# A fused attention, GLU and MLP kernel on one core: the second block's split moved ahead of the last half product, a third staging tile, other places for token sums and weight work

## The chip, the cores and the metric

One NeuronCore of one Trainium2 chip runs the whole program. The metric is the device time of one execution in microseconds, as the median of the runs; lower is better. The names of the engines are those of the profile: PE (TensorE), DVE (VectorE), ACT (ScalarE), POOL (GpSimd), SP (SyncE, here a queue for DMAs).

## What is computed

```python
phi = lambda x: exp(h - max(h)) / sqrt(128)        # h = x @ omega.T - |x|^2 / 2
x  = attention(phi(q), phi(k), v)                  # (4, 8, 576, 64) -> 2304 tokens x 512
xn = x / sqrt(mean(x * x) + 1e-6) * rms_g
x  = (silu(xn @ w_gate) * (xn @ w_val)) @ w_out    # 512 -> 1536 -> 512, the GLU
out = silu(x @ w2_in) @ w2_out                     # 512 -> 2048 -> 512, the MLP
```

All data are float32. A product of two float32 matrices is made of three passes of a rounded type (high times high, high times low, low times high), so every operand is split once into a high part (an ACT copy that rounds) and a low part (a DVE subtraction).

## The kernel before

The 2304 tokens are five blocks: 0 to 3 of 512 tokens and block 4 of 256. Behind the attention, `stream()` (L748) writes out the order of the GLU's and MLP's work as a generator; each `yield` ends a piece of PE work of a known length, and the weight queue `wq` uses these lengths to place its own jobs (decoding a weight tile on DVE, L146 to L157, adding its two halves on POOL, L160, scaling it on ACT, L168, splitting it on ACT L457 and DVE L461, adding weight tiles on POOL, L357). A call of `wq.tick()` issues one job. All engines take their instructions in the order in which they are issued.

The GLU's hidden width is cut in twelve tiles `f`. The first three are done block by block ("the third f", in the order 1, 0, 2, 3, 4); the other nine, u = 0 to 8, go by `quad()` (L593), which makes gate and value of two blocks at once, for blocks 0 and 1 (p = 0) and then for blocks 2 and 3 (p = 1), with seven half products (L595, six matmuls of 128x512 each) in place of eight; for this it needs sums of the tokens' halves (`token_sums`, L365: L382 the low parts, L379 the high ones, L387 and L390 the sums) and of the weights. In a quad the two blocks' results are `t11` and `t12`; L627 adds, L622 is the silu, L685 is `t12 * t22` of the second block where p = 1, L693 the same product where p = 0, L690 is `t11 * pb` of the first block, and L198 (ACT) and L199 (DVE) are the split of the result in `hs`. L607 copies a partial sum of one PSUM tile into the next, which the following half product continues. Block 4 has its own `glu_block` (L205 matmuls, L719 silu, L716 product, and the split is put off in a list `wait` until the next quad's first half product).

A result tile `hs` then goes through the output weights: `g2_glu` (L247, matmuls L264), four pieces of 12 or 6 matmuls for each block; other work is woven between the pieces (`more()`, `pend`). Blocks 3 and 4 are added up in SBUF (L284, DVE). Blocks 0, 1 and 2 have no room there: a piece is copied from PSUM to a staging tile (L275 on ACT, L277 on DVE, two pieces in one tile) and a POOL DMA adds it to a copy in DRAM (`kept`, L278). There are two staging tiles, used in turn, so a copy waits until the DMA that read its tile two earlier is done. Behind the last GLU group the copies come back to SBUF as the MLP's input; L254 splits them. The MLP's first group, "std", is done block by block.

Of the kernel before, what the change touches and what calls it, by code (L numbers as in the profile page):

```python
# [20 lines left out]
def kernel(  # L21
# [84 lines left out]
    f = 0  # L106
# [140 lines left out]
    def g2_glu(fs, j, hs, first, last):  # L247
        wq.need(*[(1, "o", f) for f in fs])
        staged = j < NE and not last
# [9 lines left out]
        for d in range(KC):  # L259
# [12 lines left out]
            if staged:  # L272
                if d % 2 == 0:
                    o = stage()
                    nc.scalar.activation(out=o[:, 0, :], in_=ps, func=AF.Copy)  # L275
                else:
                    nc.vector.tensor_copy(out=o[:, 1, :], in_=ps)  # L277
                    nc.gpsimd.dma_start(  # L278
                        out=kept(j, d // 2), in_=o.rearrange("p t d -> p (t d)"), accum_op=ALU.add
                    )  # L280
            elif first:
                nc.scalar.activation(out=y[:, d, :], in_=ps, func=AF.Copy)
            else:
                nc.vector.tensor_tensor(out=y[:, d, :], in0=ps, in1=y[:, d, :], op=ALU.add)  # L284
            if last:
# [78 lines left out]
    def token_sums(p, temp, end, eng=nc.vector):  # L364
# [3 lines left out]
        def tok_high(n, x):  # L368
            if n == 1:
                tok[p, n] = [xs[2 * p + 1][:, a, :KH, :] for a in range(2)]  # L370
            elif p:
                v = big.tile([P, KC * TB * P], F32R, tag=f"ya{n - 2}", name=f"ya{n - 2}")
# [40 lines left out]
    class WeightQueue:  # L413
# [28 lines left out]
        def plan(self, u):  # L442
# [82 lines left out]
            elif std <= u < std + NSTD:  # L525
# [8 lines left out]
                    (0, lambda: dec(bs[1], 1), lambda: load(u + 1, 1, 1)),  # L534
                    (1, lambda: hi(a0)),
                    (0, lambda: lo(a0)),
                    (0, lambda: dec(bs[0], 0), lambda: load(u + 1, 0, 0)),
# [63 lines left out]
    def quad(u, ys, hs, p=0, skip=0, done=True):  # L601
# [41 lines left out]
        while wait:  # L643
            wait.pop(0)()
# [25 lines left out]
        if kind == 2:  # L670
            silu(t22, t22)
            hs[j1][fs[1]] = split_h(t22, j1)
        yield from more(gap)
# [5 lines left out]
        silu(t12, t12)  # L679
        if kind == 2:  # L680
            hs[j1][fs[0]] = split_h(t12, j1)
        wq.tick()
        yield from more(gap)
        if kind == 1 and p:
            nc.vector.tensor_tensor(out=t12, in0=t12, in1=t22, op=ALU.mult)  # L685
            hs[j1][fs[0]] = split_h(t12, j1)
        yield step
        product(w2, KH, summed(p, 4), pb, False)
        if kind == 1:
            nc.vector.tensor_tensor(out=t11, in0=t11, in1=pb, op=ALU.mult)  # L690
            hs[j0][fs[0]] = split_h(t11, j0)
            if not p:
                nc.vector.tensor_tensor(out=t12, in0=t12, in1=t22, op=ALU.mult)  # L693
            yield from ys
            if not p:
                hs[j1][fs[0]] = split_h(t12, j1)
# [4 lines left out]
        wq.tick()  # L701
# [43 lines left out]

    def chain_of(*its):
# [3 lines left out]
    def stream():  # L750
        f0, (f2,) = sweeps[0][1], sweeps[1][1]
        for j in range(NE):
            for n in range(2):
                nc.sync.dma_start(out=kept(j, n), in_=ya[j][:, 1024 * n:1024 * (n + 1)])
        pend = ()
        order = [(3, f0), (4, f0), (1, [f2]), (0, [f2]), (2, [f2]), (3, [f2]), (4, [f2])]
# [20 lines left out]
        for n, (j, fs) in enumerate(order):  # L777
            hs, mine = {}, n == len(order) - 1
            for f in fs:
                yield from g1_glu(f, j, hs, () if mine else pend)  # L780
                pend = pend if mine else ()
            if n == 2:
                sums.extend(later)
                wq.free += [(0, k) for k in range(6)]
                wq.slot(("t", 1))
                stages[:] = [wq.slot(("y", k), F32) for k in range(2)]
                wq.held["t", 0] = 1, 1
                now, later = sums23()
                sums.extend(now[:9])
            out = g2_glu(fs, j, hs, j >= NE and fs is f0, False)  # L790
            pend = chain_of(pend, out) if mine else out
        sums.extend(now[9:] + later)
        wq.free.append((1, 0))
        for u, (kind, fs) in enumerate(groups):
# [6 lines left out]
            if std <= u < std + NSTD:  # L801
# [40 lines left out]
                continue  # L842
            yield from quad(u, iter(pend), hs, int(done), done=False)
# [4 lines left out]
            if kind == 1:  # L848
                out_of = lambda j: g2_glu(fs, j, hs[j], False, done)
                if done:  # L850
                    wq.release(("y", 0), ("y", 1))
                    for j in (2, 0, 1):
# [834 lines left out]
```

## Time and profile before

| | |
|---|---|
| median of 3 runs | 992.53 us (993.13, 989.47, 992.53) |
| the profiled execution | 991.23 us, of which its span 989.5 us |
| PE busy | 942.9 us, 95% |
| DVE, ACT, POOL busy | 711.3, 527.9, 470.6 us |
| mean granted TensorE clock | 0.985 |

The page's rows give for each engine its busy time, and for each wait the engine and line that ended it. A timeline row gives the start, the length, the engine, the line, output and inputs, the count, and in brackets the idle time in front of it with what ended it. PEclk is the granted TensorE clock as a share of full speed, 2.4 GHz; at 0.50 it is 1.2 GHz.

### The profile page before, as it was taken

The page shows a single profiled execution, that of the slowest core. Times are in us where ns is not written, and L with a number is a line of the kernel's source. Part 1 is how long each engine was busy: PE and PEld are TensorE (multiplying, and loading weights), DVE is VectorE, ACT ScalarE, POOL GpSimd, SP SyncE. Part 2 cuts the span into 40 slices and gives each one's busy share as a digit, 9 for nine tenths or more (in the row PEclk, how much of TensorE's full clock was granted, in tenths as well). Part 3 has the DMA queues.
Part 4 walks back from the last instruction along what each step waited for, and adds up shares of the span by engine and source line. Part 5 has one row for each costly group of instructions (what it writes and reads, how often), then busy time and mean ns, then how long its engine had stood idle before and what let it go on. Part 6 is the DMA issues. An engine that isn't in the chain of part 4 may idle for free.

```text
span 989.5 us, 17410 instructions
## 1 busy us (share of the span) xinstructions
PE 942.9 (95%) x6480; PEld 778.8 (79%) x6480; DVE 711.3 (72%) x1329; ACT 527.9 (53%) x1151; POOL 470.6 (48%) x495
## 2 busy tenths in 40 slices
PE   8999999999789999999999979999999999999998
PEld 6888878887577777777777757888888888888886
DVE  6998999658666876776776687989666666575633
ACT  6999786544344444354454435565645454545442
POOL 8887744335334344344344332636445454454411
PEclk9999999998899999999999989999999999999999
DMA  7654445137038367367467561355777786878777
GB/s 193 162 145 130 133 129 166 46 83 151 22 68 183 81 121 172 80 127 167 89 128 158 107 203 43 107 174 103 160 135 158 122 170 125 170 134 170 112 150 163
DMA packets 98789, 129.66 MB, mean 131 GB/s; under 512 B 29456, under 2 KB 75792, under 8 KB 98704
## 3 DMA queue, kind: packets, MB, share of 16 engines
q0 software_dynamic: 17280, 59.78, 34.6%
q1 hardware_dynamic: 81152, 68.70, 24.1%
q8 instruction: 51, 0.84, 0.4%
q14 instruction: 34, 0.28, 0.1%
q10 hardware_dynamic: 272, 0.07, 0.0%
HBM read 54.59 MB, written 69.21 MB: 125 GB/s over the span
## 4 chain that ended last, share of the span: by engine, by line
PE 74%; DVE 11%; ACT 5%; issue 4%; DMA 4%; POOL 1%; SPq 1%; DVEq 0%; POOLq 0%; ACTq 0%
PE g L595 23%; PE y L314 20%; PE y L264 8%; PE g L205 6%; PE y L205 3%; PE b L1155 3%; DMA out_dram<-w 3%; PE b L205 2%; ACT h L198 2%; PE b L1555 2%; PE b L1339 2%; PE kv L1235 1%; DVE w L461 1%; DVE h L199 1%; PE b L1128 1%
## 5 line engine op out<-in xcount | busy, mean ns | idle before, releaser
L160 POOL TENSOR_TENSOR m<-m,raw 128x512 int32<-128x512 int32 x136 | 198.2, 1458 | 232.7 <-DVE m L157 141.1
L314 PE MATMUL y<-w,h 128*128 128x512 f32 (+1 forms) x870 | 212.1, 388 | 0.2 <-ACT h L198 0.2
L595 PE MATMUL g<-xs,w 128*128 128x512 f32 x720 | 186.3, 396 | 7.4 <-DVE xs L382 6.2
L314 PEld LDWEIGHTS y<-w,h 128*128 128x128 f32 x870 | 161.9, 188 | 34.3 <-ACT h L198 0.7
L264 PE MATMUL y<-h,w 128*128 128x512 f32 (+1 forms) x648 | 158.9, 377 | 12.3 <-DVE h L199 4.0
L199 DVE TENSOR_TENSOR h<-s,h 128x512 fp32r<-128x512 f32 (+1 forms) x134 | 107.9, 815 | 83.8 <-ACT h L198 83.1
L595 PEld LDWEIGHTS g<-xs,w 128*128 128x128 f32 x720 | 136.3, 191 | 36.7 <-DVE xs L382 6.5
L264 PEld LDWEIGHTS y<-h,w 128*128 128x128 f32 x648 | 115.0, 192 | 44.0 <-DVE h L199 7.0
L198 ACT ACTIVATE h<-s 128x512 fp32r<-128x512 f32 (+1 forms) x134 | 77.8, 585 | 81.4 <-DVE s L690 32.5
L339 POOL DMA_DIRECT2D out_dram<-ya x64 | 58.9, 981 | 118.0 <-DVE ya L333 49.3
L205 PE MATMUL g<-xs,w 128*128 128x512 f32 x336 | 82.3, 396 | 4.1 <-ACT w L457 4.1
L461 DVE TENSOR_TENSOR w<-m,w 128x512 fp32r<-128x512 f32 x74 | 71.3, 964 | 19.3 <-ACT w L457 19.3
L331 ACT ACTIVATE ya<-y 128x512 f32<-128x512 f32 x82 | 48.2, 594 | 69.3 <-PE y L314 62.1
L278 POOL DMA_DIRECT2D out_dram<-w x54 | 48.6, 900 | 68.4 <-ACT w L275 25.9
L1204 ACT ACTIVATE e<-b,nb 128x128 f32<-128x128 f32 x272 | 75.8, 422 | 7.6 <-issue 4.2
L595 PE MATMUL g<-ya,w 128*128 128x512 f32 x270 | 69.8, 394 | 9.4 <-ACT g L607 9.4
L333 DVE COPY ya<-y 128x512 f32<-128x512 f32 x52 | 35.8, 688 | 58.7 <-PE y L314 58.7
L205 PEld LDWEIGHTS g<-xs,w 128*128 128x128 f32 x336 | 63.9, 192 | 17.7 <-ACT w L457 4.3
L595 PE MATMUL g<-w,w 128*128 128x512 f32 x270 | 70.2, 396 | 4.6 <-ACT g L607 4.6
L607 ACT ACTIVATE g<-g 128x512 f32<-128x512 f32 x60 | 34.9, 582 | 70.2 <-PE g L595 69.6
L622 ACT ACTIVATE s<-s 128x512 f32<-128x512 f32 x42 | 26.6, 632 | 83.8 <-DVE s L627 83.8
L595 PEld LDWEIGHTS g<-ya,w 128*128 128x128 f32 x270 | 50.5, 189 | 22.6 <-ACT g L607 12.3
(137 smaller groups left out, 1570.3 us busy)
## 6 DMA issues: line engine op xcount, KB each, us to landing
out_dram<-w POOLq DMA_DIRECT2D x56, 512.0 KB, 6.8
out_dram<-ya POOLq DMA_DIRECT2D x52, 512.0 KB, 6.8
raw<-in_moe_w_out_dram SPq DMA_DIRECT2D x28, 512.0 KB, 4.3
raw<-in_moe_w_in_dram SPq DMA_DIRECT2D x16, 512.0 KB, 4.3
out_dram<-ya SPq DMA_DIRECT2D x14, 512.0 KB, 4.9
raw<-in_moe_w_gate_dram SPq DMA_DIRECT2D x12, 512.0 KB, 4.2
raw<-in_moe_w_val_dram SPq DMA_DIRECT2D x12, 512.0 KB, 4.2
qT<-e SPq DMA_DIRECT2D x72, 64.0 KB, 2.4
```

Of the source, the lines that this page charges most:

```text
L160: tt(out=mi, in0=mi, in1=(low if step == 5 else high).bitcast(I32), op=ALU.add)
L198: nc.scalar.activation(out=ht[:, 0, :], in_=s, func=AF.Copy)
L199: nc.vector.tensor_tensor(out=ht[:, 1, :], in0=s, in1=ht[:, 0, :].bitcast(F32), op=ALU.subtract)
L205: nc.tensor.matmul(out=ps, lhsT=w[:, a, cc * P:(cc + 1) * P], rhs=xs[j][:, c, cc, :], start=(n == 0), stop=(n == 3 * KC - 1),)
L264: nc.tensor.matmul(out=ps, lhsT=wt[1, "o", f][:, a, d * P:(d + 1) * P], rhs=hs[f][:, c, :], start=(n == 0), stop=(n == nn - 1),)
L278: nc.gpsimd.dma_start(out=kept(j, d // 2), in_=o.rearrange("p t d -> p (t d)"), accum_op=ALU.add)
L314: nc.tensor.matmul(out=ps, lhsT=hs[f][:, a, t * P:(t + 1) * P], rhs=wt[2, "p", f][:, c, d0:d1], start=(n == 0), stop=(n == nn - 1),)
L331: nc.scalar.activation(out=o[:, t % 2, :], in_=ps, func=AF.Copy)
L339: nc.gpsimd.dma_start(out=rows, in_=o[p0:p1], accum_op=ALU.add)
L461: eng.tensor_tensor(out=v[:, 1, :], in0=x, in1=v[:, 0, :].bitcast(F32), op=ALU.subtract)
L595: nc.tensor.matmul(out=ps, lhsT=w[:, a, (c0 + c) * P:(c0 + c + 1) * P], rhs=x(b, c), start=(start and n == 0), stop=(n == 3 * KH - 1), ski ...
L1204: nc.scalar.activation(out=st.e[r][:, :, h, :] if blocks4 else st.e[r][:, h, :], in_=src.rearrange("p (a f) -> p a f", a=4) if blocks4 els ...
```

## The change

1. The third f's output of block 1 is added in SBUF (four L284) as block 3's is, and stored by two plain POOL DMAs; only blocks 0 and 2 are stored at the start of `stream()`, and block 1's two staged accumulations at that place are gone.
2. The sums of tokens of blocks 2 and 3 are issued one block sooner (at `n == 1`), into tiles that are free there, with other tags; those of blocks 0 and 1 that are left stand in front of them, and `wq.rest` is 1.3 and then 2.1.
3. In `quad`, `t12 * t22` and the split of the second block stand right behind the sixth half product for both p. Before, for p = 0, the product stood behind the seventh half product and the first block's split, and the split behind the output pieces. The weight job that stood behind the sixth half product stands behind the fifth, and that at the quad's end is issued in fewer cases.
4. There are three staging tiles from u = 1 on instead of two. Block 4's split stands behind block 1's output pieces, and the pieces of a group come in the order 1, 2, 4 instead of 1, 4, 2; in the last GLU group the order of blocks is 2, 1, 0, 4 instead of 2, 0, 1, 4.
5. In std the decode of a second output weight tile stands one split later.

Where the lines moved: L595, L607, L622, L627, L690 and L693, L457, L461, L379, L382, L387, L390 of before are L599, L611, L626, L631, L693 and L685, L460, L464, L382, L385, L390, L393 of the changed kernel. PE has the same instructions.

DVE, where the third f of block 1 is put out and that of block 0 computed (`ya_96`: block 1's output in SBUF; `w_1` and `w_2`: staging tiles; `ya_97`: token sums; L228 and L199: block 0's product and its low part, for which PE waits). Before:

```order
L277 COPY w_1_3947<-y 128x512
L382 TENSOR_TENSOR xs_91<-raw_3715,xs_91 128x1024
L146 TENSOR_SCALAR m_3979<-raw_3911 128x512
L149 TENSOR_SCALAR raw_3911<-raw_3911 128x512
L152 TENSOR_SCALAR m_3979<-m_3979 128x512
L154 TENSOR_SCALAR raw_3911<-raw_3911 128x512
L157 TENSOR_SCALAR m_3979<-m_3979 128x512
L277 COPY w_2_3948<-y 128x512
L387 TENSOR_TENSOR ya_97<-xs_93 128x1024
L228 TENSOR_TENSOR s<-s,g 128x512
L199 TENSOR_TENSOR h<-s,h 128x512
```

DVE at the same place in the changed kernel (`w_1` is a sum of tokens here):

```order
L284 TENSOR_TENSOR ya_96<-y,ya_96 128x512
L385 TENSOR_TENSOR xs_91<-raw_3713,xs_91 128x1024
L146 TENSOR_SCALAR m_3977<-raw_3903 128x512
L149 TENSOR_SCALAR raw_3903<-raw_3903 128x512
L152 TENSOR_SCALAR m_3977<-m_3977 128x512
L154 TENSOR_SCALAR raw_3903<-raw_3903 128x512
L157 TENSOR_SCALAR m_3977<-m_3977 128x512
L284 TENSOR_TENSOR ya_96<-y,ya_96 128x512 x3
L393 TENSOR_TENSOR ya_97<-ya_97 128x1024
L393 TENSOR_TENSOR ya_97<-ya_97,w_1_3922 128x1024
L228 TENSOR_TENSOR s<-s,g 128x512
L199 TENSOR_TENSOR h<-s,h 128x512
```

Two staging copies are four additions now, and two sums of 128x1024 stand in front of block 0's product in place of one.

DVE in one period of the nine GLU groups (u = 4), first quad, from the second of the two additions (L627) on; `raw` and `m` are a weight tile before and after its decode. Before:

```order
L627 TENSOR_TENSOR s<-g,e 128x512
L461 TENSOR_TENSOR w_3_5561<-m_5479,w_3_5561 128x512
L146 TENSOR_SCALAR m_5601<-raw_5283 128x512
L149 TENSOR_SCALAR raw_5283<-raw_5283 128x512
L152 TENSOR_SCALAR m_5601<-m_5601 128x512
L154 TENSOR_SCALAR raw_5283<-raw_5283 128x512
L157 TENSOR_SCALAR m_5601<-m_5601 128x512
L277 COPY w_1_3947<-y 128x512
L690 TENSOR_TENSOR s<-s,g 128x512
L199 TENSOR_TENSOR h<-s,h 128x512
L693 TENSOR_TENSOR s<-s 128x512
L277 COPY w_2_3948<-y 128x512
```

DVE in the changed kernel, from behind the first of the two additions (L631) on; `ya_3690` is block 4's output:

```order
L464 TENSOR_TENSOR w_5_5558<-m_5479,w_5_5558 128x512
L146 TENSOR_SCALAR m_5583<-raw_5265 128x512
L149 TENSOR_SCALAR raw_5265<-raw_5265 128x512
L152 TENSOR_SCALAR m_5583<-m_5583 128x512
L154 TENSOR_SCALAR raw_5265<-raw_5265 128x512
L157 TENSOR_SCALAR m_5583<-m_5583 128x512
L277 COPY w_0_4520<-y 128x512
L631 TENSOR_TENSOR s<-g,e 128x512
L685 TENSOR_TENSOR s<-s 128x512
L199 TENSOR_TENSOR h<-s,h 128x512
L284 TENSOR_TENSOR ya_3690<-y,ya_3690 128x256 x2
L693 TENSOR_TENSOR s<-s,g 128x512
```

The decode (L146 to L157) and its split, which stood behind both additions, stand in front of the second, and the second block's product and low part (L685, L199) are in front of the first block's (L693, L199) and no longer behind.

ACT in the same period, second quad, from two staging copies (L275) to block 4's silu (L719). Before:

```order
L275 ACTIVATE w_1_3947<-y 128x512
L275 ACTIVATE w_2_3948<-y 128x512
L622 ACTIVATE s<-s 128x512
L168 ACTIVATE m_5647<-m_5647,g_sb 128x128 x4
L457 ACTIVATE w_1_5741<-m_5647 128x512
L198 ACTIVATE h<-s 128x512 x2
L719 ACTIVATE s<-y 128x256
```

ACT at the same place in the changed kernel (L626 is the second silu):

```order
L275 ACTIVATE w_2_3951<-y 128x512
L168 ACTIVATE m_5647<-m_5647,g_sb 128x128 x4
L460 ACTIVATE w_0_5721<-m_5647 128x512
L275 ACTIVATE w_3_3952<-y 128x512
L626 ACTIVATE s<-s 128x512
L198 ACTIVATE h<-s 128x512 x2
L719 ACTIVATE s<-y 128x256
```

The scaling of a weight tile (L168 four times) and its high part (L460), which stood between the second silu and the two L198, stand in front of that silu.

The core of the diff:

```diff
     def g2_glu(fs, j, hs, first, last, keep=None):
-        staged = j < NE and not last
+        staged = j < NE and not last and keep is None
...
+            if keep and d % 2:
+                keep(j, d // 2)
...
     def tok_high(n, x):
             elif p:
-                v = big.tile([P, KC * TB * P], F32R, tag=f"ya{n - 2}", name=f"ya{n - 2}")
+                tag = f"ya{(1, 0, 2)[n - 2]}"
+                v = big.tile([P, KC * TB * P], F32R, tag=tag, name=tag)
...
     def quad(u, ys, hs, p=0, skip=0, done=True):
         product(w1, 0, half(0, 0), pa, True)
         copy(pb, pa)
-        while wait:
-            wait.pop(0)()
...
         product(s34, 0, summed(p, 3), pb, False)
         t22 = plus(pb)
         if kind == 2:
             silu(t22, t22)
             hs[j1][fs[1]] = split_h(t22, j1)
+        else:
+            wq.tick()
         yield from more(gap)
         yield step
         product(s34, KH, half(1, KH), pc, False)
...
         t12 = plus(pc)
         silu(t12, t12)
+        if kind == 1:
+            nc.vector.tensor_tensor(out=t12, in0=t12, in1=t22, op=ALU.mult)
+        hs[j1][fs[0]] = split_h(t12, j1)
         if kind == 2:
-            hs[j1][fs[0]] = split_h(t12, j1)
-        wq.tick()
+            wq.tick()
         yield from more(gap)
-        if kind == 1 and p:
-            nc.vector.tensor_tensor(out=t12, in0=t12, in1=t22, op=ALU.mult)
-            hs[j1][fs[0]] = split_h(t12, j1)
         yield step
         product(w2, KH, summed(p, 4), pb, False)
         if kind == 1:
             nc.vector.tensor_tensor(out=t11, in0=t11, in1=pb, op=ALU.mult)
             hs[j0][fs[0]] = split_h(t11, j0)
-            if not p:
-                nc.vector.tensor_tensor(out=t12, in0=t12, in1=t22, op=ALU.mult)
             yield from ys
-            if not p:
-                hs[j1][fs[0]] = split_h(t12, j1)
...
-        wq.tick()
+        if kind == 2 or not done:
+            wq.tick()
...
     def stream():
-        for j in range(NE):
+        for j in (0, 2):
...
+        wq.rest = 1.3
...
-            wq.rest = T_PACE if wq.hold else S_REST
+            wq.rest = 2.1
...
+            if n == 1:
+                wq.free += [(0, k) for k in range(4)]
+                for k in range(2):
+                    wq.slot(("t", k), F32)
+                now, later23 = sums23()
+                sums.extend(now)
             if n == 2:
-                sums.extend(later)
+                sums[:0] = later
...
-                sums.extend(now[:9])
+            if n == 5:
+                sums.extend(later23)
...
+            if u == 1:
+                stages.insert(0, wq.slot(("y", 2), F32))
...
                 yield from glu_block(fs[0], 4, hs[4], iter(()), {"g": 0, "v": 0})
+                wq.tick()
                 if done:
-                    pend = chain_of(*map(out_of, (2, 0, 1, 4)))
+                    pend = chain_of(*map(out_of, (2, 1, 0, 4)))
                 else:
                     yield from out_of(3)
-                    pend = chain_of(*map(out_of, (2, 1, 4) if u + 2 == std else (1, 4, 2)))
+                    pend = chain_of(out_of(1), flush(), out_of(2), out_of(4))
```

## Rows read from the trace of the kernel before

**Rows 1.** The page's busy times: engine, us, share of the span, instructions.

```profile
PE 942.9 (95%) x6480; PEld 778.8 (79%) x6480; DVE 711.3 (72%) x1329; ACT 527.9 (53%) x1151; POOL 470.6 (48%) x495
```

**Rows 2.** Waits of PE: what it waited for, us in total, times, longest.

```profile
PE g L595 <- ACT g L607: 14.0, 8, 4.6
PE g L595 <- DVE xs L382: 6.2, 1, 6.2
```

**Rows 3.** Timeline of PE, third f and first quads, rows with idle time in front.

```profile
219.04 0.50 PE L264 MATMUL y<-h,w 128*128 128x512 f32 x1 [0.53 <-ACT h L198]
...
229.75 0.50 PE L264 MATMUL y<-h,w 128*128 128x512 f32 x1 [1.75 <-ACT h L198]
...
230.87 3.35 PE L264 MATMUL y<-h,w 128*128 128x512 f32 x7 [0.62 <-DVE h L199]
...
264.88 2.50 PE L595 MATMUL g<-xs,w 128*128 128x512 f32 x5 [6.15 <-DVE xs L382]
...
283.33 2.06 PE L264 MATMUL y<-h,w 128*128 128x512 f32 x6 [1.93 <-ACT s L719]
```

**Rows 4.** Windows: stretch, length, busy time of each engine, then the granted clock.

```profile
230.90:237.00 6.10, 6.10 (x14) 4.76 (x15) 4.31 (x6) 2.44 (x4) 3.08 (x3) 0.50 0.93 154
...
261.50:267.10 5.60, 2.22 (x5) 1.83 (x6) 5.01 (x12) 0.00 (x0) 3.27 (x1) 0.50 0.00 0
...
284.60:288.10 3.50, 3.50 (x10) 2.77 (x9) 1.99 (x4) 0.11 (x1) 0.00 (x0) 0.54 0.00 0
...
300.00:570.00 270.00, 253.77 (x1202) 206.27 (x1201) 189.37 (x340) 121.70 (x248) 115.32 (x114) 1.00 0.61 127
574.90:581.90 7.00, 5.96 (x14) 4.70 (x15) 4.75 (x9) 3.05 (x6) 2.59 (x2) 0.51 0.18 71
```

**Rows 5.** Timeline of DVE, third f: the sum ahead of block 0's product, and that product.

```profile
215.78 1.95 DVE L387 TENSOR_TENSOR ya<-xs 128x1024 f32<-128x1024 f32 x1
217.65 0.68 DVE L228 TENSOR_TENSOR s<-s,g 128x512 f32<-128x512 f32 x1
```

**Rows 6.** Timeline of ACT, third f: the staging copy ahead of block 2's split.

```profile
226.61 0.60 ACT L275 ACTIVATE w<-y 128x512 f32<-128x512 f32 x1 [3.60 <-DMA out_dram<-w]
```

**Rows 7.** Timeline of PE in one period, from the second quad on.

```profile
421.67 1.67 PE L595 MATMUL g<-ya,w 128*128 128x512 f32 x6 [1.34 <-ACT g L607]
...
431.36 2.99 PE L205 MATMUL y<-xs,w 128*128 128x256 f32 x24
434.19 0.39 PE L264 MATMUL y<-h,w 128*128 128x512 f32 x1
...
438.74 1.54 PE L595 MATMUL g<-xs,w 128*128 128x512 f32 x6
```

**Rows 8.** Timeline of DVE in the same period, first quad's end.

```profile
413.57 0.69 DVE L627 TENSOR_TENSOR s<-g,e 128x512 f32<-128x512 f32 x1 [0.75 <-PE g L595]
...
418.43 1.43 DVE L199 TENSOR_TENSOR h<-s,h 128x512 fp32r<-128x512 f32 x1 [0.70 <-ACT h L198]
419.79 0.68 DVE L693 TENSOR_TENSOR s<-s 128x512 f32<-128x512 f32 x1
```

**Rows 9.** Timeline of POOL: the decode's pair of additions beside that L199.

```profile
416.63 2.69 POOL L160 TENSOR_TENSOR m<-m,raw 128x512 int32<-128x512 int32 x2 [6.52 <-DVE m L157]
```

**Rows 10.** Timeline of ACT in the same period: the scaling ahead of the two L198.

```profile
431.46 1.27 ACT L168 ACTIVATE m<-m,g_sb 128x128 f32<-128x128 f32 x4
432.76 0.63 ACT L457 ACTIVATE w<-m 128x512 fp32r<-128x512 f32 x1
```

**Rows 11.** Timeline of PE at the end of the GLU: its two longest waits there.

```profile
575.95 2.50 PE L595 MATMUL g<-w,w 128*128 128x512 f32 x5 [4.60 <-ACT g L607]
...
595.44 2.06 PE L205 MATMUL g<-xs,w 128*128 128x512 f32 x4 [4.08 <-ACT w L457]
```

**Rows 12.** Timeline of ACT ahead of those two: a staging copy, and the first block's split.

```profile
566.95 0.60 ACT L275 ACTIVATE w<-y 128x512 f32<-128x512 f32 x1 [1.87 <-DMA out_dram<-w]
...
594.24 0.63 ACT L198 ACTIVATE h<-s 128x512 fp32r<-128x512 f32 x1 [2.44 <-DVE s L693]
```

More of the change, by code (lines that the diff above doesn't have):

```diff
@@ L245, in kept, with g2_glu @@
         return out[r0:r0 + 2 * P, :].rearrange("(p r) d -> p (r d)", r=2)
-    def g2_glu(fs, j, hs, first, last):
+    def g2_glu(fs, j, hs, first, last, keep=None):
         wq.need(*[(1, "o", f) for f in fs])
-        staged = j < NE and not last
+        staged = j < NE and not last and keep is None
         y = ya[j].rearrange("p (c t) -> p c t", c=KC)
@@ L533, in plan @@
                     (0, lambda: lo(a1)),
-                    (0, lambda: dec(bs[1], 1), lambda: load(u + 1, 1, 1)),
+                    *[(0, lambda: dec(bs[1], 1), lambda: load(u + 1, 1, 1))] * (u > std),
                     (1, lambda: hi(a0)),
                     (0, lambda: lo(a0)),
+                    *[(0, lambda: dec(bs[1], 1), lambda: load(u + 1, 1, 1))] * (u == std),
                     (0, lambda: dec(bs[0], 0), lambda: load(u + 1, 0, 0)),
@@ L744, in take, with flush @@
                 yield c
+    def flush():
+        while wait:
+            wait.pop(0)()
+        yield from ()
     def chain_of(*its):
@@ L751, in stream, with keep @@
         f0, (f2,) = sweeps[0][1], sweeps[1][1]
-        for j in range(NE):
+        def keep(j, n):
+            (nc.gpsimd if j == 1 else nc.sync).dma_start(out=kept(j, n), in_=ya[j][:, 1024 * n:1024 * (n + 1)])
+        for j in (0, 2):
             for n in range(2):
-                nc.sync.dma_start(out=kept(j, n), in_=ya[j][:, 1024 * n:1024 * (n + 1)])
+                keep(j, n)
         pend = ()
+        wq.rest = 1.3
         order = [(3, f0), (4, f0), (1, [f2]), (0, [f2]), (2, [f2]), (3, [f2]), (4, [f2])]
@@ L781, in stream @@
                 pend = pend if mine else ()
+            if n == 1:
[4 more added lines that the diff above has]
+                sums.extend(now)
             if n == 2:
-                sums.extend(later)
-                wq.free += [(0, k) for k in range(6)]
-                wq.slot(("t", 1))
+                sums[:0] = later
+                wq.free += [(0, 4), (0, 5)]
                 stages[:] = [wq.slot(("y", k), F32) for k in range(2)]
-                wq.held["t", 0] = 1, 1
-                now, later = sums23()
-                sums.extend(now[:9])
-            out = g2_glu(fs, j, hs, j >= NE and fs is f0, False)
+            if n == 5:
+                sums.extend(later23)
+            out = g2_glu(fs, j, hs, j >= NE and fs is f0, False, keep if j == 1 else None)
             pend = chain_of(pend, out) if mine else out
-        sums.extend(now[9:] + later)
-        wq.free.append((1, 0))
+        wq.free += [(1, 0), (1, 1)]
         for u, (kind, fs) in enumerate(groups):
@@ L850, in stream @@
                 if done:
-                    wq.release(("y", 0), ("y", 1))
-                    for j in (2, 0, 1):
+                    wq.release(*[("y", k) for k in range(3)])
+                    for j in (2, 1, 0):
                         ya[j] = big.tile([P, KC * TB * P], F32, tag=f"ya{j}", name=f"ya{j}")
```

## The prediction

> **What bounds the kernel now.** I read the page's busy times first: PE works 942.9 us of a span of 989.5 [rows 1], so only the idle time of PE (46.6 us) and the stretches in which its clock is down can be won; its instructions stay the same. Second, the waits of PE: one line, the copy L607 from PSUM to PSUM, ends 14.0 us of waiting in eight places, and one low part of token sums (L382) ends a single wait of 6.2 us [rows 2]. Third, the timeline of PE around those waits: the reader is to see that the first five stand between 219 and 284 us, in the third f and the first pair of quads [rows 3], that a short one returns in every period of the nine groups [rows 7], and that two long ones stand at the GLU's end [rows 11]. Fourth, the windows: the granted clock is 1.00 from 300 to 570 us although PE stops for 1.34 us seven times there, but it is 0.50 to 0.54 (1.2 GHz) in a stretch behind each longer stop [rows 4]. So a longer wait costs twice, once itself and once in the clock. Behind the 1.93 us wait the clock was at 0.54 for 3.5 us, which is 1.6 us lost; I use 1.6 as the price of one fall, and the border lies between 1.34 and 1.93.
>
> The sum is made against the profiled execution (991.2 us); the median of the runs stands 1.3 above it. About 0.5% (5 us) is what a measurement of this kernel can tell from no change.
>
> **Third f and first pair of quads (changes 1, 2, 4).**
> - Block 0's output pieces. DVE now does four additions where two staging copies stood (two more at about 0.6 us), and two 1024-wide sums in front of block 0's product L228 in place of one. The one there took 1.95 us beside POOL's decode, a plain one 1.2 or so, so L228 comes about 2 us behind its 217.65 [rows 5], and the wait of 0.53 behind it [rows 3] grows to about 2.6. Ends: 1.2 more (the sums do not wait for POOL) and 3.4 more (both do). Above the border, so a fall of the clock goes with it: +2.1 +1.6.
> - Block 2's split. ACT stood 3.60 us for a staging tile that its DMA still read [rows 6], and the split behind it let PE wait 1.75 and 0.62 us [rows 3]; then the clock was at 0.50 for 6.1 us [rows 4]. With block 1 added in place there is no DMA of block 1 in front of these tiles, and ACT and DVE have four staging copies less. The waits and the fall go: -2.4 and -3.0. If a wait of under 1 us stays in its place, it costs no clock.
> - The sums of blocks 2 and 3. The low part of block 3 (xs) that PE waited for during 6.15 us stands before the first quad now; its fall of the clock (2.22 us of work at 0.50 [rows 4]) goes too. In its place I take 1.0 us for a sum that is still late: -5.2 and -1.1.
> - What was hidden under those 6.15 us: the second block's chain, which now ends on the path that the period's copy waits for. Block 4's narrow pieces leave PE less to do there than in the later periods, and I take the wait at the third half product of the second quad at 3.5 us, with a fall: +3.5 +1.6. Ends: 1.3 without a fall (what a later period shows) and 5.
> - The 1.93 us wait for block 4's silu (L719) [rows 3]. L168 and its high part stand one product sooner, and ACT comes to L719 sooner: about 0.8 is left, under the border: -1.1 -1.6.
>
> Sum of this part: -5.6, and between -9 and -1 by the ends.
>
> **Seven periods (changes 3 and 4).** Two places matter in each.
> - *Third half product of the second quad*, 421.67 with 1.34 in front [rows 7]: PE wanted it at 420.33. Before, the chain was the first block's product, split, second block's product at 419.79, then L198, the copy L607 and PE, 1.88 us from that product's start to PE [rows 8, 7]. Now the second block goes first, but behind the decode and its L277, and the last product is the first block's. Twenty-four 256-wide matmuls took 2.83 us [rows 7], six 0.71, six 512-wide ones twice that; with block 2's pieces in front of block 4's two such steps are longer, so the second addition is ready 1.4 us later than 413.57 [rows 8], at 415.0; DVE is still in the decode and I take 415.6 (between 415.0 and 416.0). Silu 0.7, then L685 at 417.0. It lies beside the decode's pair of POOL additions, 2.69 us for two, 1.35 each [rows 9]. The L199 of 418.43 took 1.43 us beside such a pair [rows 8] where others take 0.7: it ended 0.5 us behind the pair's end. The decode has moved about 1.5 us forward, and so has the pair, to about 415.1 to 417.8; L685 then ends at 418.3, L198 and L199 of the second block take till 419.7, two narrow additions till 420.3, and 1.88 us behind that PE starts at 422.2: a wait of 1.9 in place of 1.34. Ends: 1.2 (L685 runs freely) and 2.4. I take 1.9, by the row of L199: +0.6, seven times +4.2.
> - *Block 3's pieces.* Twelve matmuls from 434.19 to 438.74 took 4.55 us [rows 7]; at 2.83 for twenty-four halves 1.7 us of that are waits. ACT scaled a weight tile in front of the two L198, to 433.4 [rows 10]; it stood behind a silu that ended about 431.5, and the product between takes 0.7. Moved in front of that silu, it lets L198 begin about 1.0 us sooner, and all behind it follows: -1.0, seven times -7.0. Ends: -0.5 and -1.3.
>
> The Trainium skill has a rule that speaks against this part: by GPSIMD Engine Reference, 1. Specifications, GpSimd shares its SBUF interfaces with VectorE, and contends with VectorE instructions that have two SBUF inputs. The row of L199 (1.43 us where others take 0.7) agrees; by the rule the second block's product pays in every period, as in the sum, and without it the wait would be 1.2 and the sum 5 us lower.
>
> Sum of this part -2.8, between -7 and +3 without a fall of the clock.
>
> **End of the GLU (changes 3, 4 and 5).** The 4.60 us wait at 575.95 [rows 11] goes back to staging copies that waited for a DMA, 1.87 us at 566.95 [rows 12]: with three tiles and block 1 before block 0 that wait is hidden, and the chain behind gains what it cost: I take 2.1, the period's wait and a little, so -2.5; the stretch at 0.51 behind it (7.0 us, 5.96 busy [rows 4], about 3.0 lost) shrinks to one fall of 1.6: -1.4. The 4.08 us wait at 595.44 [rows 11] was for a weight's high part behind the L198 of 594.24 [rows 12], itself behind the second block's product; this goes first now, but the weight's low part on DVE follows: 3.2 is left, -0.9. Together -4.8, between -7 and -2. POOL's queue has two accumulating DMAs less and SP two plain ones less, in front of nothing late: nothing.
>
> **Sum:** 991.2 - 5.6 - 2.8 - 4.8 = 978.0 for a profiled execution, and with the 1.3 of the median 979. The likeliest case's own range is 971 to 986.
>
> **The rivals.**
> 1. *The clock falls in every period.* The wait of 1.9 is what the wait of 283.33 was, behind which the clock fell [rows 3, 4]. Then each period pays 1.6 more: 7 x 1.6 = 11, and 979 becomes 990; if it falls in some periods, 982 to 988. For: the one row of that length. Against: all seven waits of 1.34 left it at 1.00, and with L685 free the wait is 1.2. [...]
> 2. *Slower: the second block's chain holds the first's.* The place is the same L685. If it waits for the whole of POOL's pair from a later start (a decode that comes 1.35 us later, because the weight job is issued with the sixth half product's addition not yet done), the first block's product comes 1.35 us later and the wait is 3.2 with a fall each time: 7 x (1.35 + 1.6) = 21, 979 becomes 1000. It decides from about 1.2 us of added delay with falls in all periods. For: in the third f a 1024-wide sum lost 0.7 us beside the pair [rows 5]. Against: no row before shows more than one POOL instruction waited out.
> 3. *The third tile does nothing.* The DMA, and not the number of tiles, sets the pace, so the 4.60 stays: 979 becomes 983 with its clock. For: the ACT copy of 226.61 waited 3.60 with the ring of two [rows 6], in a stretch with the DMAs close. Against: in the periods PE never waits for a staging copy.
>
> **How the numbers follow.** Forecast 0.50, rival 1 0.27 (a third of that below 987.5), rival 2 0.12, rival 3 0.11. Faster by over 0.5% (below 987.5): 0.50 x 0.96 + 0.09 + 0.11 = 0.68; within 0.5%: 0.20; slower: 0.12. The range leaves out the best of the forecast's ends and rival 2: 968 to 994.
>
> **What would show it.** In the changed profile: no wait above 1.5 us for xs; a wait of about 2.6 at block 0's pieces near 221; waits for the copy L611 near 1.9 in each period, with the windows' clock at 1.00 there (0.5 would be rival 1); L685 beside POOL's L160 at over 1.2 us (0.7 would make the period's wait 1.2); twelve matmuls of block 3 in about 3.5 us instead of 4.55; the copy's longest wait about 3.5, no more 4.6 at the end. Wrong it would be with waits of over 3 us in each period, or with the waits gone at one place and back at the next output pieces.

## The result, and the profile after

The changed kernel takes 980.55 us (median of 4 runs, 976.76 to 981.29) against 992.83 before: a ratio of 0.9875, 95% interval 0.9841 to 0.9909. The profiled execution has 980.27 us and a span of 978.5, which is 11.0 less than before. The forecast was 979, in a range of 968 to 994.

The waits of PE in the profile after (what it waited for, us in total, times, longest), which answer to [rows 2]:

```profile
PE g L599 <- ACT g L611: 20.6, 10, 3.3
PE y L264 <- DVE s L716: 3.3, 8, 0.4
PE y L264 <- ACT h L198: 3.2, 2, 2.5
PE g L205 <- DVE w L464: 3.0, 1, 3.0
PE y L264 <- DVE ya L284: 2.3, 2, 1.8
```

The long single wait for xs is gone; waits for the copy (L611, L607 before) are more, and each is shorter than 3.4. Where they stand is seen in the timeline of PE after, rows with idle time in front from 205 to 310 us and at the GLU's end; it answers to [rows 3] and [rows 11]:

```profile
221.78 0.50 PE L264 MATMUL y<-h,w 128*128 128x512 f32 x1 [2.50 <-ACT h L198]
...
231.37 0.50 PE L264 MATMUL y<-h,w 128*128 128x512 f32 x1 [0.66 <-ACT h L198]
232.50 2.79 PE L264 MATMUL y<-h,w 128*128 128x512 f32 x11 [0.63 <-DVE h L199]
...
247.56 2.14 PE L599 MATMUL g<-w,w 128*128 128x512 f32 x6 [2.01 <-ACT g L611]
...
265.25 2.65 PE L599 MATMUL g<-ya,w 128*128 128x512 f32 x6 [3.34 <-ACT g L611]
...
304.29 1.65 PE L599 MATMUL g<-ya,w 128*128 128x512 f32 x6 [1.91 <-ACT g L611]
...
566.53 1.67 PE L599 MATMUL g<-w,w 128*128 128x512 f32 x6 [1.91 <-ACT g L611]
...
582.68 1.80 PE L205 MATMUL g<-xs,w 128*128 128x512 f32 x4 [3.00 <-DVE w L464]
...
598.13 1.66 PE L264 MATMUL y<-h,w 128*128 128x512 f32 x6 [1.75 <-DVE ya L284]
```

And one period of PE, which answers to [rows 7]; the row at 432.89 is the end of block 3's pieces, as 438.74 is there, and the last row is where the next period's like wait ends:

```profile
416.66 1.67 PE L599 MATMUL g<-ya,w 128*128 128x512 f32 x6 [1.90 <-ACT g L611]
...
426.36 2.99 PE L205 MATMUL y<-xs,w 128*128 128x256 f32 x24
429.19 2.50 PE L264 MATMUL y<-h,w 128*128 128x512 f32 x9
432.09 0.96 PE L264 MATMUL y<-h,w 128*128 128x512 f32 x3 [0.41 <-DVE s L716]
432.89 1.53 PE L599 MATMUL g<-xs,w 128*128 128x512 f32 x6
...
454.13 1.67 PE L599 MATMUL g<-ya,w 128*128 128x512 f32 x6 [1.90 <-ACT g L611]
```

The like row of the next period before:

```profile
459.42 0.97 PE L595 MATMUL g<-ya,w 128*128 128x512 f32 x3 [1.33 <-ACT g L607]
```

Three places make up the 11.0 us. Up to the row at 432.89, which stood at 438.74, 5.85 are won. A period is 37.47 long (416.66 to 454.13) in place of 37.75 (421.67 to 459.42), 0.28 less, and four of the seven (four of the waits, and block 3's pieces four times) lie before that row: 1.12. So the third f and the first quads brought 4.7, the seven periods 2.0, and the end of the GLU the rest, 4.3: the wait of 4.60 is 1.91 now, that of 4.08 is 3.00, and a new one of 1.75 has come.

Why the period's wait grew from 1.34 to 1.90 is seen on DVE and POOL, in their timelines after, one after the other; the rows answer to [rows 8] and [rows 9]:

```profile
409.40 0.69 DVE L277 COPY w<-y 128x512 f32<-128x512 f32 x1
410.00 0.68 DVE L631 TENSOR_TENSOR s<-g,e 128x512 f32<-128x512 f32 x1
411.44 1.37 DVE L685 TENSOR_TENSOR s<-s 128x512 f32<-128x512 f32 x1 [0.76 <-ACT s L626]
...
414.78 0.68 DVE L693 TENSOR_TENSOR s<-s,g 128x512 f32<-128x512 f32 x1
```

```profile
409.57 2.69 POOL L160 TENSOR_TENSOR m<-m,raw 128x512 int32<-128x512 int32 x2 [1.85 <-DVE m L157]
```

L685 is issued at 411.44, while the second addition of POOL's pair runs; it ends at 412.81, 0.55 behind the pair.

The granted clock, windows of the profile after (stretch, length, busy time of each engine, clock), answers to [rows 4]:

```profile
221.00:234.00 13.00, 10.71 (x44) 8.11 (x45) 11.61 (x16) 8.92 (x18) 6.69 (x6) 1.00 0.65 186
...
247.00:252.00 5.00, 4.44 (x12) 3.53 (x13) 4.13 (x5) 2.12 (x5) 1.16 (x1) 0.66 0.34 105
...
264.00:270.00 6.00, 4.75 (x14) 3.75 (x15) 2.42 (x7) 3.66 (x9) 2.61 (x2) 0.72 0.07 25
...
300.00:566.00 266.00, 248.42 (x1187) 203.30 (x1185) 190.72 (x341) 122.69 (x248) 117.60 (x113) 1.00 0.62 127
```

Behind the 1.90 of the periods it stayed at 1.00; behind 2.01 and 3.34 it fell, and behind the 3.00 at 582.68 too (0.63 from 582 to 586 us); behind the 2.50 at 221.78 it did not.

### The profile page after: what moved, and what is told of

Read it like the earlier page. It is cut to its first block, busy times and chain, and to the rows that moved or that the text cites. A ratio compares the mean times of both kernels' runs of the same rounds, so it can differ in the third digit from the quotient of the medians.

```text
span 978.5 us, 17362 instructions
## 1 busy us (share of the span) xinstructions
PE 936.8 (96%) x6480; PEld 775.0 (79%) x6480; DVE 715.4 (73%) x1331; ACT 528.2 (54%) x1149; POOL 469.1 (48%) x495
## 4 chain that ended last, share of the span: by engine, by line
PE 64%; DVE 14%; ACT 5%; issue 3%; DVEq 0%; ACTq 0%
PE g L599 23%; PE y L316 20%; PE y L264 8%; PE g L205 5%; PE y L205 3%; ACT h L198 3%; DVE h L199 2%; DVE s L685 2%; DVE w L464 2%; DVE ya L284 2%; PE b L1571 1%; PE b L205 1%; DVE s L631 1%; ACT s L626 1%; DVE s L693 1%
## 5 line engine op out<-in xcount | busy, mean ns | idle before, releaser
L160 POOL TENSOR_TENSOR m<-m,raw 128x512 int32<-128x512 int32 x136 | 193.4, 1423 | 250.1 <-DVE m L157 126.9
L599 PE MATMUL g<-xs,w 128*128 128x512 f32 x720 | 182.8, 391 | 0.0
L199 DVE TENSOR_TENSOR h<-s,h 128x512 fp32r<-128x512 f32 (+1 forms) x134 | 100.6, 761 | 96.2 <-ACT h L198 96.0
L264 PE MATMUL y<-h,w 128*128 128x512 f32 (+1 forms) x648 | 156.1, 374 | 9.6 <-DVE s L716 3.3
L599 PEld LDWEIGHTS g<-xs,w 128*128 128x128 f32 x720 | 134.8, 189 | 28.3 <-DVE w L464 0.3
L198 ACT ACTIVATE h<-s 128x512 fp32r<-128x512 f32 (+1 forms) x134 | 77.9, 586 | 84.6 <-DVE s L693 33.9
L599 PE MATMUL g<-ya,w 128*128 128x512 f32 x270 | 70.7, 398 | 16.7 <-ACT g L611 16.7
L464 DVE TENSOR_TENSOR w<-m,w 128x512 fp32r<-128x512 f32 x74 | 74.5, 1006 | 15.7 <-ACT w L460 15.7
L205 PE MATMUL g<-xs,w 128*128 128x512 f32 x336 | 81.4, 392 | 3.2 <-DVE w L464 3.0
L205 PEld LDWEIGHTS g<-xs,w 128*128 128x128 f32 x336 | 62.8, 189 | 16.9 <-DVE w L464 3.4
L599 PEld LDWEIGHTS g<-ya,w 128*128 128x128 f32 x270 | 50.5, 190 | 30.3 <-ACT g L611 20.1
L599 PE MATMUL g<-w,w 128*128 128x512 f32 x270 | 69.5, 393 | 3.9 <-ACT g L611 3.9
L611 ACT ACTIVATE g<-g 128x512 f32<-128x512 f32 x60 | 34.9, 581 | 69.5 <-PE g L599 68.9
L278 POOL DMA_DIRECT2D out_dram<-w x52 | 44.9, 863 | 56.7 <-issue 24.6
L626 ACT ACTIVATE s<-s 128x512 f32<-128x512 f32 x42 | 26.5, 632 | 77.1 <-DVE s L631 77.1
```

The costliest lines, as they stand in the source:

```text
L160: tt(out=mi, in0=mi, in1=(low if step == 5 else high).bitcast(I32), op=ALU.add)
L198: nc.scalar.activation(out=ht[:, 0, :], in_=s, func=AF.Copy)
L199: nc.vector.tensor_tensor(out=ht[:, 1, :], in0=s, in1=ht[:, 0, :].bitcast(F32), op=ALU.subtract)
L205: nc.tensor.matmul(out=ps, lhsT=w[:, a, cc * P:(cc + 1) * P], rhs=xs[j][:, c, cc, :], start=(n == 0), stop=(n == 3 * KC - 1),)
L264: nc.tensor.matmul(out=ps, lhsT=wt[1, "o", f][:, a, d * P:(d + 1) * P], rhs=hs[f][:, c, :], start=(n == 0), stop=(n == nn - 1),)
L278: nc.gpsimd.dma_start(out=kept(j, d // 2), in_=o.rearrange("p t d -> p (t d)"), accum_op=ALU.add)
```

## The experiments

The theory: the weight job's place decides, since it sets what stands in front of the second block's product on DVE and what POOL runs beside it; the early split itself is a cost. The rival: the early split brings the gain. Diffs are against the changed kernel unless said; times are medians of 4 to 10 runs beside the kernel before on the same chip (991.8 to 992.8).

**The weight job behind the sixth half product again.**

```diff
-        else:
-            wq.tick()
         yield from more(gap)
...
         silu(t12, t12)
         if kind == 1:
+            wq.tick()
             nc.vector.tensor_tensor(out=t12, in0=t12, in1=t22, op=ALU.mult)
```

> The changed kernel with one thing undone: the weight job stands behind the sixth half product's silu again, in front of the second block's product L685, and no longer behind the fifth. Theory (the decode and POOL's pair beside L685 set the period's wait of 1.90 us): the second addition is no longer late (409.3 instead of 410.0 in the period from 395.43), but the low part and the decode, 2.3 us, now stand between it and L685, which begins at about 412 as a free one of 0.7 us; it ends where it ends now (412.8) and L199 behind it is the one that waits for POOL. The wait stays at 1.9 to 2.5 and the time at 980 to 985. Rival (the place of the weight job is what made the change faster): the wait goes to 3 or more and the time to 988 or more.

Measured: 995.92 us, ratio to before 1.0021 (1.0002 to 1.004); the change without this one line gains nothing. The chain was as the theory had it, but the time was the rival's: the wait is mostly 2.23, only 0.33 longer, and the clock falls behind it in five of the eight periods. A row of PE's timeline and windows of two such places:

```profile
541.41 1.70 PE L599 MATMUL g<-ya,w 128*128 128x512 f32 x6 [2.24 <-ACT g L611]
```

```profile
541.00:546.00 5.00, 4.59 (x14) 3.65 (x15) 3.27 (x9) 3.55 (x9) 1.91 (x2) 0.69 0.35 105
581.00:586.00 5.00, 4.35 (x19) 3.62 (x20) 4.54 (x9) 2.83 (x6) 1.66 (x2) 1.00 0.34 105
```

The edit moves the job in the second quad too, and block 3's pieces wait 0.43 twice again, as before. A period with a fall is 40.25 long (302.89 to 343.14), one without 38.60 (343.14 to 381.74). So the price that rival 1 of the prediction set on a fall is real, 1.65 where 1.6 was taken, and five of them are some 8 of the 15 us; a period without one is 1.13 longer than in the change, of which the wait is 0.33 and block 3's pieces the rest.

**The weight job behind the fourth half product.**

```diff
         t11 = silu(pa, s_tile())
         wq.tick()
+        if kind == 1 and not done:
+            wq.tick()
...
-        else:
+        elif done:
             wq.tick()
```

> The changed kernel, but in the first quad of each group the weight job that stood behind the fifth half product stands behind the fourth, so decode and POOL's pair come 1.5 to 2.2 us sooner. Theory (the wait of 1.90 us in each period is the decode in front of the second addition, 0.7, and POOL's pair beside L685, another 0.7): L685 falls to 0.7 us, the wait for the copy L611 to 0.5 in the periods, and from 3.34 to about 2 in the first group; the time falls by 9 x 1.4, to 968 to 971. Rival (the wait is the length of the chain of two splits itself and not POOL): the wait stays above 1.5 and the time above 977.

Measured: 967.6 us, ratio 0.9735 (0.9702 to 0.9769). The second block's product is free of POOL, and the wait falls to 0.65 (timelines of DVE, then PE):

```profile
402.23 0.69 DVE L687 TENSOR_TENSOR s<-s 128x512 f32<-128x512 f32 x1 [0.76 <-ACT s L626]
```

```profile
261.99 1.65 PE L599 MATMUL g<-ya,w 128*128 128x512 f32 x6 [1.46 <-ACT g L611]
...
406.77 1.66 PE L599 MATMUL g<-ya,w 128*128 128x512 f32 x6 [0.65 <-ACT g L611]
```

The two halves of the theory (decode in front of the addition, pair beside the product) move together here; L685's 1.37 against 0.69 is POOL's half.

**The split late again.**

```diff
-        if kind == 1:
+        if kind == 1 and p:
             nc.vector.tensor_tensor(out=t12, in0=t12, in1=t22, op=ALU.mult)
-        hs[j1][fs[0]] = split_h(t12, j1)
+        if kind == 2 or p:
+            hs[j1][fs[0]] = split_h(t12, j1)
...
             hs[j0][fs[0]] = split_h(t11, j0)
+            if not p:
+                nc.vector.tensor_tensor(out=t12, in0=t12, in1=t22, op=ALU.mult)
             yield from ys
+            if not p:
+                hs[j1][fs[0]] = split_h(t12, j1)
```

> The changed kernel with the headline edit undone for the first quad: the second block's product and split stand behind the seventh half product and the first block's split again; the weight jobs, the three tiles and all else stay as changed. Theory (the early product is what puts L685 beside POOL's pair; the decode's new place does the good): the chain behind the second addition is first product, split, second product, split, all behind POOL's pair, and the wait for the copy L611 falls from 1.90 to about 0.6; time 968 to 973. Rival (the early split shortens the chain before the third half product): the wait grows to 2.5 or more, the clock falls, and the time is 985 or more.

Measured: 966.64 us, ratio 0.974 (0.9712 to 0.9767): without its headline edit in the first quads the change is 14 us faster. The wait is 0.46 in the periods. The product that now comes first, L694, has one input in PSUM; it runs inside POOL's pair and takes 0.69, where L685, with both inputs in SBUF, took 1.37 beside the pair in the change. So the order of the two products decides which of them meets the pair, and what that costs (timelines of PE, DVE, POOL):

```profile
403.71 1.66 PE L599 MATMUL g<-ya,w 128*128 128x512 f32 x6 [0.46 <-ACT g L611]
```

```profile
399.83 0.69 DVE L694 TENSOR_TENSOR s<-s,g 128x512 f32<-128x512 f32 x1
```

```profile
398.06 2.69 POOL L160 TENSOR_TENSOR m<-m,raw 128x512 int32<-128x512 int32 x2 [1.85 <-DVE m L157]
```

**Each of the two edits alone, on the kernel before.** The weight job:

```diff
             hs[j1][fs[1]] = split_h(t22, j1)
+        else:
+            wq.tick()
...
             hs[j1][fs[0]] = split_h(t12, j1)
-        wq.tick()
+            wq.tick()
```

> The kernel before with one edit of the change alone: in the GLU's quads the weight job stands behind the fifth half product instead of the sixth; split, tiles, sums and orders stay as before. Theory (the weight job's place is what the periods gain from, the early split costs): L199 of the first block no longer lies beside POOL's pair and the wait of 1.34 falls to 0.5 to 0.8; in the second quad the scaling no longer stands in front of the two L198, and block 3's pieces win 1.0; nine periods of 1.5 to 1.8, and the early and late waits (6.15, 4.60) stay: time 976 to 980, as much as the whole change. Rival (the job's place alone only moves the wait): 988 to 993.

Measured: 971.33 us, ratio 0.9787 (0.9771 to 0.9804), 9 us below the whole change. In the periods the copy is not waited for at all, in PE's timeline:

```profile
411.59 1.66 PE L595 MATMUL g<-ya,w 128*128 128x512 f32 x6
```

The period is 35.41 (391.61 to 427.02, rows of block 3's pieces). And the split, at its new place in both quads:

```diff
         wq.tick()
+        if kind == 1:
+            nc.vector.tensor_tensor(out=t12, in0=t12, in1=t22, op=ALU.mult)
+            hs[j1][fs[0]] = split_h(t12, j1)
         yield from more(gap)
...
-            if not p:
-                nc.vector.tensor_tensor(out=t12, in0=t12, in1=t22, op=ALU.mult)
             yield from ys
-            if not p:
-                hs[j1][fs[0]] = split_h(t12, j1)
```

> The kernel before with the headline edit alone: in the first quad too the second block's product and split stand right behind the sixth half product; weight jobs, tiles, sums and orders stay as before. Theory (the early split by itself saves nothing, since the first block's product becomes the last of the chain and waits for the second's low part beside POOL's pair): L199 of the second block takes 1.4, the wait at the third half product is 1.5 to 2.3 in place of 1.34, and where it passes 2 the clock falls; time 993 to 1006. Rival (the early split is a gain that the weight job's place only adds to): the wait falls under 1.2 and the time to 986 or less.

Measured: 992.83 us, ratio 0.9992 (0.9979 to 1.0005). The wait is 1.42 in place of 1.34; the low part of the second block took 1.02 beside POOL, and the clock stayed up. Alone the split is worth nothing, the weight job 21 us.

**Two staging tiles.**

```diff
-            if u == 1:
-                stages.insert(0, wq.slot(("y", 2), F32))
...
-                    wq.release(*[("y", k) for k in range(3)])
+                    wq.release(*[("y", k) for k in range(2)])
```

> The changed kernel with two staging tiles instead of three. Theory (the third tile hides the wait of the staging copies for their DMAs): ACT's copies L275 wait 1 to 3 us for DMAs again, the second addition comes later in the first quad, and PE's wait at the end of the GLU goes from 1.91 to 3 or more; time 982 to 986. Rival (the third tile does nothing, the order of the blocks is what took the wait of 4.60 away): end wait 1.9, time 980 to 981.

Measured: 1006.7 us, ratio 1.0124 (1.0084 to 1.0164), 20 us above the theory's figure. The place was not only the GLU's end. In seven of eight periods ACT waits for DMAs at two copies (timeline of ACT), the second addition is late, PE's wait is 3.14, and the clock falls in seven of eight periods (timeline of PE, then a window behind it):

```profile
415.43 0.60 ACT L275 ACTIVATE w<-y 128x512 f32<-128x512 f32 x1 [2.48 <-DMA out_dram<-w]
417.91 0.60 ACT L275 ACTIVATE w<-y 128x512 f32<-128x512 f32 x1 [1.88 <-DMA out_dram<-w]
```

```profile
426.18 2.93 PE L599 MATMUL g<-ya,w 128*128 128x512 f32 x6 [3.15 <-ACT g L611]
```

```profile
426.00:431.00 5.00, 4.82 (x14) 3.89 (x15) 2.71 (x8) 2.47 (x8) 2.12 (x2) 0.66 0.36 70
```

**Two tiles, block 4's pieces ahead of block 2's again**, beside the edit above:

```diff
-                    pend = chain_of(out_of(1), flush(), out_of(2), out_of(4))
+                    pend = chain_of(out_of(1), flush(), out_of(4), out_of(2))
```

> The run with two staging tiles, with the pieces in the order 1, 4, 2 again instead of 1, 2, 4. Theory (block 2 right behind block 1 asks for four tiles in a row, and only that made the third tile necessary): the copies wait for no DMA in front of the second addition, the wait goes from 3.14 back to 1.9 or less, and the time from 1006.7 to 978 to 984. Rival (two tiles are too few under the early split in any order): time above 990.

Measured: 1000.6 us, ratio 1.0079 (1.0053 to 1.0105). The period's wait went to 1.70 as the theory had it, but the time is the rival's, since block 4's split now stands right in front of its own pieces, and PE waits there too, in each of eight periods:

```profile
412.06 1.32 PE L264 MATMUL y<-h,w 128*128 128x256 f32 x6 [1.57 <-ACT h L198]
```

Whether two tiles would do with that split further ahead is open; it wasn't tried.

**Block 1 through staging tiles again.**

```diff
-        for j in (0, 2):
+        for j in range(NE):
...
-            out = g2_glu(fs, j, hs, j >= NE and fs is f0, False, keep if j == 1 else None)
+            out = g2_glu(fs, j, hs, j >= NE and fs is f0, False, None)
```

> The changed kernel with the first edit undone: the third f's output of block 1 goes through staging tiles and accumulating DMAs again, and all three blocks are stored at the start. Theory (block 2's wait and the fall of the clock behind it came from the DMAs of block 1 in front of the staging tiles): the wait of 2.49 at block 0's pieces shrinks to about 1, but ACT waits 3 us for a tile before block 2's split and PE 1.8 or more with a fall of the clock; time 981 to 985. Rival (the additions in DVE cost at block 0 what they save at block 2): time 976 to 980.

Measured: 980.7 us, ratio 0.9889 (0.9858 to 0.9921), as with the change. The waits change places, 0.50 at block 0's pieces and 2.19 at block 2's, in place of 2.50 and 0.66, and a fall of the clock comes with the second (0.72 from 232 to 238 us):

```profile
221.89 0.51 PE L264 MATMUL y<-h,w 128*128 128x512 f32 x1 [0.50 <-ACT h L198]
...
233.05 0.65 PE L264 MATMUL y<-h,w 128*128 128x512 f32 x1 [2.19 <-ACT h L198]
```

**The sums of blocks 2 and 3 one block later.** The block under `n == 1` stands under `n == 2`, behind the rest of the first sums:

```diff
-            if n == 1:
+            if n == 2:
+                sums.extend(later)
                 wq.free += [(0, k) for k in range(4)]
...
-            if n == 2:
-                sums[:0] = later
```

> The changed kernel with the sums of blocks 2 and 3 issued one block later, as before (their tiles and the pace stay as changed). Theory (the wait of 6.15 us went because these sums were issued sooner): a wait of 2 to 6 us for a token sum of blocks 2 and 3 returns in the first pair of quads, and hides most of the 3.34 there; the two sums in front of block 0's product are gone, and the wait of 2.49 with them; time 979 to 983. Rival (the pace, 1.3 and 2.1 for 1.2 and 2.1, did it): no wait for sums, and the time 976 to 979.

Measured: 986.11 us, ratio 0.9936 (0.9918 to 0.9953), 5.6 above the change. Block 0's wait falls from 2.50 to 1.21, but block 2's grows from 0.66 to 2.43. The wait for xs is back, and a weight that stands behind the sums is late too:

```profile
247.00 0.73 PE L599 MATMUL g<-xs,w 128*128 128x512 f32 x2 [3.29 <-ACT w L460]
...
267.32 2.50 PE L599 MATMUL g<-xs,w 128*128 128x512 f32 x5 [3.89 <-DVE xs L385]
```

**The MLP's first weight sooner.**

```diff
-        if kind == 2:
+        if kind == 2 or done and u + 1 == std:
             wq.tick()
```

> The changed kernel, but in the last GLU group's second quad the low part of the MLP's first weight stands behind the second block's split and not at the end of the group. Theory (the wait of 3.00 us at 582.68 is DVE's order alone): the low part is done 2.0 us sooner, the wait falls to about 1, the clock stays at 1.00 there and saves some 1.6 more; time 976.5 to 978. Rival (the wait moves to the MLP's first output pieces, which need the splits that are now later): time 979.5 to 981.5.

Measured: 981.98 us, ratio 0.9882 (0.9849 to 0.9914): nothing. The rival: the wait of 3.00 is 0.21, and four waits of 1.35 to 1.67 stand at the next output pieces, where the change has 1.75 and 0.58; two of them here:

```profile
579.66 1.20 PE L205 MATMUL g<-xs,w 128*128 128x512 f32 x4 [0.21 <-DVE w L464]
...
585.94 0.96 PE L264 MATMUL y<-h,w 128*128 128x512 f32 x3 [1.67 <-DVE s L716]
...
604.67 1.22 PE L264 MATMUL y<-h,w 128*128 128x256 f32 x6 [1.65 <-DVE ya L284]
```

**The first block's split behind the copy**, on the run with the weight job behind the fourth:

```diff
         copy(pb, pa)
+        settle()
         yield from more()
...
-            hs[j0][fs[0]] = split_h(t11, j0)
+            splits.append(lambda: hs[j0].update({fs[0]: split_h(t11, j0)}))
             yield from ys
...
                 yield from glu_block(fs[0], 4, hs[4], iter(()), {"g": 0, "v": 0})
+                settle()
                 wq.tick()
```

Here `settle()` issues what stands in the list `splits` and empties it.

> The run with the decode behind the fourth half product, and the first block's split (L198, L199) put off in every quad of the GLU: behind the next quad's first copy L611, and behind block 4's product in the second quad. Theory (what is left at the third half product, 0.65, is the copy queued behind the first block's split on ACT, and the 0.42 and more at block 3's pieces is L716 queued behind that split on DVE): both waits go, a period falls from 36.20 to 34.9 to 35.2, and the time to 956 to 959. Rival (the waits move to the output pieces, which now get their split late): period 36 or more, time 966 or more.

Measured: 947.77 us, ratio 0.9563 (0.9539 to 0.9587), the fastest here, 8 us below the lowest figure expected. Between 300 and 550 us the timeline of PE lists one wait alone, for the MLP's first weight behind the last period, and PE is busy for 248.43 of 250 (the row, then the window):

```profile
548.76 1.20 PE L205 MATMUL g<-xs,w 128*128 128x512 f32 x4 [1.57 <-DVE w L464]
```

```profile
300.00:550.00 250.00, 248.43 (x1225) 210.57 (x1224) 192.42 (x356) 126.03 (x248) 120.40 (x112) 1.00 0.68 145
```

**The same with slower sums at the start.**

```diff
-        wq.rest = 1.3
+        wq.rest = 1.5
```

> The kernel of the run before with wq.rest 1.5 instead of 1.3 at the start, which leaves one 1024-wide sum in front of block 0's product L228 instead of two. Theory (the wait of 2.49 at block 0's pieces is these two sums beside POOL): the wait falls to 1 or less, the clock stays at 1.00 there, and the time is 3 to 4.5 us under that of the run before. Rival (the sums that come later hold the first quad): the waits at 247 and 262 grow by as much; within 1 us of the run before.

Measured: 948.34 us, ratio 0.9565 (0.9546 to 0.9584). The wait at block 0's pieces is 0.54, but waits of 1.35 and 1.03 for a weight come at 242 and 244: the rival.

## Why the prediction was right, and where not

- *Third f and first quads.* Foretold -5.6, measured -4.7. The steps held: block 0's wait 2.6 against 2.50, xs gone, 3.5 against 3.34 in the first group, no fall of the clock behind block 2's wait. Sizes were off and in part cancelled, which is luck: no fall behind the 2.50 in this execution, though six of the experiments' profiles have one behind the like wait; the wait for block 4's silu gone, where 0.8 was to be left; against that 2.01 with a fall at 247.56 where 1.0 without one stood, and 0.66 and 0.63 left at block 2's pieces, where the sum had both waits gone. That change 1 pays for itself is not shown: with it undone the time is the same. The sums are worth some 5.6.
- *Seven periods.* Foretold -2.8, measured -2.0. The third half product's wait was foretold at 1.9 and is 1.90, and the chain is the one foretold: PE wanted that product at 420.33 before and at 414.76 now, and with these 5.57 us added the second addition starts at 415.57 (415.6 was taken), L685 ends at 418.38 (418.3) and the first block's product starts at 420.35 (420.3). L685 beside POOL took 1.37, by the row of L199 that the sum used. Block 3's twelve pieces were foretold at about 3.5 us and take 3.70 (429.19 to 432.89): 0.85 won in each period and not 1.0. The clock stayed up as the likeliest case had it, but rival 1 was near: it fell behind five of eight waits of 2.23 to 2.57 in one run, and once behind 1.91 in another.
- *The end.* Foretold -4.8, measured -4.3. The wait of 4.60 went to 1.91 (2.1 was taken) and that of 4.08 to 3.00 (3.2). No fall of the clock was left behind the 1.91 (1.00 from 566 to 574 us), where the sum kept one, and a new wait of 1.75 at 598.13 was not in the sum. What the third tile, the order of the blocks and change 5 each did here is open: with two tiles the wait of 1.91 is 3.15, with two and the old order of pieces 1.71, and change 5 was not tried alone.
- *What the sum did not see* is what each edit is worth alone. Rival 3 priced the third tile at 4 us; without it the changed kernel is 26 us slower, because under the new order of the pieces the tile carries every period and not the end alone. And the +0.6 that the sum booked for the period's wait was the small visible part of the early split's cost: with the split back, the weight job's new place takes that wait from 1.90 to 0.46. The sum compared the wait with 1.34, and not with what the wait would be under the other edits.
- Rival 2 (slower) did not happen in the change. In the run with the weight job behind the sixth the decode came later, as that rival had it, and the time is 15 us longer; but there L685 is free (0.68) and the low part behind it pays (1.01), so that the wait grew by 0.33 and not by 1.35.

## What to carry to other kernels

Price the edits of a bundle against the kernel that has all the others, not against the kernel before: here one moved line was worth 21 us alone, the edit that gave the change its name nothing alone and 14 lost beside the others. Look for what stands on an in-order engine in front of the one copy that the matmuls wait for, and move it behind that copy: a weight's decode by one product and a split by one copy gave 33 us more than the change. A wait close to those behind which the clock fell should be taken as a risk with a price, here 1.65 us for each fall.

## What the runs showed of the hardware

The clock did not go by the wait in front of a stretch alone. 1.90 and 1.91 left it at 1.00 in the eight periods of the change, but behind one wait of 1.91, at 564.74 in the run with the MLP's first weight sooner, the window from 564 to 570 has 0.72; waits of 2.23 to 2.57 let it fall in five of eight periods with the weight job behind the sixth, and three of 2.23 there did not; the 2.50 at block 0's pieces left it up in the change (1.00 from 220 to 232 us), and waits of 2.48 and 2.49 there let it fall in six of the experiments' profiles (0.86 in the same stretch). What decides among like waits stays open.

What DVE pays beside POOL's pair depended on the instruction: a product with both inputs in SBUF took 1.37 in place of 0.69, one with an input in PSUM 0.69. A decode step, which has one SBUF input and takes 0.42 us at 582.54, took 1.47 and 1.52 where it was issued beside the pair, in the profile after (DVE, then POOL):

```profile
584.55 1.47 DVE L146 TENSOR_SCALAR m<-raw 128x512 uint32<-128x512 uint32 x1
585.95 1.52 DVE L149 TENSOR_SCALAR raw<-raw 128x512 uint32<-128x512 uint32 x1
```

```profile
584.44 2.74 POOL L160 TENSOR_TENSOR m<-m,raw 128x512 int32<-128x512 int32 x2 [12.27 <-issue]
```
